# Gated mix of linear attention and a long convolution: taps constant over all lags, and the sum onto y on GpSimd

## The chip, the cores and the metric

The kernel runs on one core of a Trainium2 chip. The metric is the device time of one launch in microseconds (us), as the median of several runs. The engines are named as in the profile: PE is TensorE (PEld its weight loads), DVE is VectorE, ACT is ScalarE, POOL is GpSimd, and SP is the queue that issues the DMAs. All of them run beside each other and wait for one another through semaphores; each takes its own instructions in the order in which they were written.

## The reference: what is computed

x has 2048 rows (time) and 448 columns (channels). A gate g mixes two blocks of the same x:

```python
x = A_x
g = _sigmoid((x * gate_w).sum(-1, keepdims=True))
a = _A_ref(x, A_wqkv, A_wo)                      # linear attention, 16 heads of 28
b = _B_ref(x, ...)                               # convolution over time, one filter per channel
return g * a + (1 - g) * b

# _A_ref, not causal: phi(t) = where(t > 0, t + 1, exp(t)) + 1e-6
kv = jnp.einsum("bhsd,bhse->bhde", phi(k), v)
o = phi(q) kv / (phi(q) sum(phi(k)) + 1e-6)      # then o @ wo

# _B_ref: causal, as long as the sequence
A = -jnp.exp(log_A_real) + 1j * A_imag           # per channel, 256 modes
K = 2.0 * einsum("dn,dnl->dl", (C_real + 1j*C_imag) * dt, exp(A * dt * lag)).real
y = causal_convolution(x, K) + x * D_skip
```

The step dt = exp(log_dt) is around 1e-14 with these inputs, so over 2048 lags a filter K hardly moves: it is p0 + p1 * lag to very high accuracy, with p0 = 2 dt sum(C_real) and a slope p1 = -2 dt^2 sum(C_real exp(log_A_real) + C_imag A_imag).

## The kernel before, in words

**Tiles.** Time is cut into NC = 16 chunks of P = 128 rows, the channels into J = 4 blocks of DJ = 112. Matrices that need full accuracy are split into a high part in fp32r and the rest ("low"); a product is then three PE products, high by high, low by high, high by low. For a chunk c, `split_x(c)` (L260) makes one tile xw: ACT casts x to fp32r (L272), GpSimd subtracts for the low part of the transposed x (512 wide) and for the low part of x in natural order (448 wide; both L258). `skip(c)` (L277, GpSimd) writes x * D_skip into y[:, c]. `load_x` (L229) brings x of a chunk, 512 KB, through SP's queue.

**The main loop** (L520, c = 1 to 14, after chunks 0 and 1 have been begun by hand) does the following on PE:

- `project(c + 1, wk)` (L370): 11 matmuls for k of the next chunk, into one PSUM buffer named k. Then `k_post` (L410): ACT does relu and exp (L396, L397), VectorE the feature (L398, in PSUM), ACT the high part pkh (L402), VectorE the low part pkl and the running sum zb (both L408). The next k may start when zb has read the buffer.
- from c = 2, `project(c, wq)`: 11 matmuls for q of this chunk, into one PSUM buffer q, and `q_post` (L415): ACT exponentials (L416, L385), VectorE L386 and L389, into pq. The next q may start after L389.
- `do_g(c)` (L438): 11 matmuls that add x^T phi(k) into four PSUM banks.
- the triangle products v of the convolution, which are off this sequence by some chunks.

**The convolution inside a chunk.** With K = p0 + p1 * lag, written as p0 (1 + slope * lag) with slope = p1 / p0, and the lag as the difference of two positions, the part of a chunk that comes from itself is tri @ (x - x * s) scaled by near, where tri is the 128 by 128 triangle of ones and s the slope times the position. `do_wa` (L451, VectorE) makes q = x * slope, `do_wb` (L455, VectorE) subtracts it from the low part of x, `do_v` (L459, L460) is two PE products with tri, `v_post` (L464, VectorE) multiplies by near and sends the last row of the chunk into u by a DMA (L467), and `v_add` (L470, VectorE) adds to y[:, c]. Lists `vs` and `vq` and the tuple TWICE decide at which c which chunk's w and v are done; from c = 4 on it is one or two chunks an iteration, and their order on each engine is the order in the code.

**The convolution between chunks.** The 15 rows of u, and ru = u times the slopes, are gathered by four DMAs into zr (L492), split into zst, and multiplied by the constant matrix gcat in `inter(i)` (L740), in two groups of 8 chunks, into rc. In the attend stage one of the 11 matmuls of a chunk takes rc, against rows phi that hold the gate and the gate times the position (six rows a chunk), put there by DMA (L640) and copied by `tail` (L672).

**The preparation of the filter**, `s4d_prepare` (L305), is a generator of steps: exp; squares on ACT and sums with accumulation on VectorE (L314, L317); then small operations on [112, 4] tiles (L321 to L342), among them the check; then eight PE transposes (L347) that spread p0 and p1 over partitions, a copy into slope (L348), into ru (L350), and near = p0 (1 + slope) (L351). The steps are called before the loop, at c = 1 after `k_post`, at c = 2 after `q_post`, and at c = 3 around `q_post`.

**The check.** For each channel okc is 1 if the modes are slow enough (md), p0 is within bounds, and |p1| * FLAT <= |p0| with FLAT = 2^23. The count of channels that pass is loaded at the end; if one fails, `general_conv` computes the convolution in full and overwrites the output (L869).

**After the loop** come the gate (L423 to L425), `gates_a` and `gates_b` (the rows phi, L647 to L658), the sum of phi(k) over time spread by PE (L707, L708) and copied (L709), the normalisation of q (`norm_a` to `norm_d`), the products with wv and wo (L775, L749, L752), and then, for each of 16 chunks, the **attend stage**: `turn` (4 transposes, L664), `attend` (11 matmuls, L686), `final_b` (L691, VectorE, and the DMA out). A generator `late` (L814) puts the second `inter` and the gate of the last chunk between these.

Of the kernel before, what the change touches and what calls it, by code (L numbers as in the profile page):

```python
# [22 lines left out]
J = 4  # L23
# [6 lines left out]
LAG = 3  # L30
WARM = 8
QA = (2, 2, 5)
TWICE = (4, 5, 6, 8, 10, 12)
SMALL = 2.0 ** -70
FLAT = 2.0 ** 23
# [3 lines left out]
RG = 8  # L39
RX = DT + 6 * RG  # L40
NZ = 2 * (NC - 1)
KZ = 32 + NZ
# [129 lines left out]
def gated_mix_kernel(ctx: ExitStack, tc: tile.TileContext, xin, wk_d, wq_d, wv_d, wo_d, abc_d, ldt_d, dsk_d,  # L172
# [26 lines left out]
    gcat = const.tile([KZ, 2, RX], F32R, name="gcat")  # L199
    sel = const.tile([P, 2], F32, name="sel")  # L200
# [3 lines left out]
    rows = const.tile([P, 3 * D], F32, name="rows")  # L204
    near, slope, dsk = (rows[:, i * D:(i + 1) * D] for i in range(3))
    ru = const.tile([NC, D], F32, name="ru")
# [9 lines left out]
    xs = work.enter_context(tc.tile_pool(name="xs", bufs=LAG + 3))  # L216
# [5 lines left out]
    POOL.memset(zb, 0.0)  # L222

# [81 lines left out]
    def s4d_prepare():  # L305
# [4 lines left out]
        s0, s1, dt, am, p0, p1, d2, md, b0, b1, nk = (small() for _ in range(11))  # L310
# [9 lines left out]
        clamp = lambda p: DVE.tensor_scalar(out=p, in0=p, scalar1=-BIG, scalar2=BIG, op0=ALU.max, op1=ALU.min)  # L320
# [8 lines left out]
        clamp(p0)  # L329
        clamp(p1)  # L330
# [13 lines left out]
        o = [ps.tile([P, 512], F32, name="p%d" % i, tag="v%d" % (1 - i)) for i in range(2)]  # L344
        for i, f in ((0, p0), (1, p1)):
            for j in range(J):
                PE.transpose(o[i][:, j * DJ:(j + 1) * DJ], f[:, j:j + 1].to_broadcast([DJ, P]), ident[:DJ, :DJ])  # L347
        ACT.activation(slope, o[1][:, :D], AF.Copy, scale=sel[:, 0:1])  # L348
        yield
        ACT.copy(ru, o[1][:NC, :D])  # L350
        DVE.scalar_tensor_tensor(out=near, in0=slope, scalar=1.0, in1=o[0][:, :D], op0=ALU.add, op1=ALU.mult)  # L351
# [89 lines left out]
    vt, wt = {}, {}  # L441

    def do_w(c, eng):
        do_wa(c)
        do_wb(c, eng)

    wq = {}

    def do_wa(c):
        q = wq[c] = tp.tile([P, D], F32, name="q", tag="t")  # L450
        DVE.tensor_tensor(out=q, in0=xh[c][:, NAT:LO].bitcast(F32), in1=slope, op=ALU.mult)  # L451

    def do_wb(c, eng):
        w = wt[c] = tp.tile([P, D], F32R, name="w", tag="w")
        eng.tensor_tensor(out=w, in0=xh[c][:, XC:LT].bitcast(F32), in1=wq.pop(c), op=ALU.subtract)  # L455

    def do_v(c):
        v = vt[c] = ps.tile([P, 512], F32, name="v", tag="v%d" % (c % 2))
        PE.matmul(v[:, :D], lhsT=tri, rhs=xh[c][:, NAT:LO], start=True, stop=False)  # L459
        PE.matmul(v[:, :D], lhsT=tri, rhs=wt.pop(c), start=False, stop=True)  # L460

    def v_post(c):
        t = tp.tile([P, D], F32, name="t", tag="v0")
        DVE.tensor_tensor(out=t, in0=vt[c][:, :D], in1=near, op=ALU.mult)  # L464
        vt[c] = t
        if c < NC - 1:
            SP.dma_start(out=u[c:c + 1], in_=t[P - 1:P])  # L467

    def v_add(c):
        DVE.tensor_tensor(out=y[:, c], in0=y[:, c], in1=vt.pop(c), op=ALU.add)  # L470
# [6 lines left out]
    vs = list(range(NC))  # L477
    vq = []

    def v_next():  # L480
        vq.append(vs.pop(0))
        do_v(vq[-1])

    U = slice(0, NC - 1)

    def z_products():
        zr = tp.tile([P, D], F32, name="zr", tag="w")[:64]
        POOL.memset(zr, 0.0)
        DVE.tensor_tensor(out=ru[U], in0=u[U], in1=ru[U], op=ALU.mult)
        for o in (0, 32):  # L490
            for k, w in enumerate((u[U], ru[U])):
                SP.dma_start(out=zr[o + k * (NC - 1):o + (k + 1) * (NC - 1)], in_=w)  # L492
# [27 lines left out]
    for c in range(1, NC - 1):  # L520
        if c == 1:
            load_x(4)
            gcr = tp.tile([P, D], F32, name="gcr", tag="w")[:KZ, :2 * RX].rearrange("p (g m) -> p g m", g=2)
# [19 lines left out]
        if c + 2 < NC and c != LAG + 1:  # L543
            split_x(c + 2)
            skip(c + 2)
# [5 lines left out]
        if vq:  # L551
            v_add(vq.pop(0))
        if c in (NC - 5, NC - 3):
            low(POOL, wol[-1], wo[:, 2 * len(wol) - 2:2 * len(wol)], woh[-1])
        if c > LAG and c >= 12 and vs[c in TWICE:]:
            do_w(vs[c in TWICE], DVE)
        k_post(c + 1, ko)
# [5 lines left out]
        if c in TWICE:  # L563
            v_next()
            v_post(vq[0])
            if c > LAG + 1:
                v_add(vq.pop(0))
        if c == LAG + 1:
            split_x(c + 2)
            v_add(vq.pop(0))  # L570
            skip(c + 2)
# [12 lines left out]
        if c == 2:  # L584
            steps(1)
# [382 lines left out]
```

## Time and profile before

| what | value |
|---|---|
| median of 3 runs | 211.92 us (210.81 to 212.89) |
| span of the profiled execution, first to last instruction | 209.6 us |
| mean granted PE clock over the span | 0.985 of full speed |
| busy: PE, DVE, POOL, ACT | 179.2, 169.4, 105.7, 94.6 us |
| first k of iteration c = 2, 3, 4, 14 of the main loop | 25.70, 32.56, 40.41, 136.05 us |
| first attend matmul of the steady attend stage | 161.35 us |

The profile shows one execution. Its own time is recorded as the span only; the median of the runs lies 2.3 us above it. A page gives busy times, the chain of work that ended last, and groups of instructions by code line: "L470 DVE TENSOR_TENSOR y<-y,t 128x448" is an instruction of line 470 on VectorE that writes a tile y from y and t; xN is the count, then follow the total busy time in us, the mean of one in ns, and how long the engine was idle before them and for whom. A timeline row starts with the start and the duration in us; neighbouring instructions of one kind are merged, with their count. A window row has the start and end, the length, each engine's busy time with its count of instructions, and the granted PE clock.

### The profile page before, as it was taken

What the parts mean: (1) busy time and instruction counts of PE and PEld (TensorE: products, weight loads), DVE (VectorE), ACT (ScalarE), POOL (GpSimd) and SP (SyncE); (2) the same over time, 40 slices, a digit from 0 to 9 for tenths busy, and PEclk for the clock granted to TensorE, in tenths of its full rate; (3) what the DMA queues carried; (4) which work ended last, traced back from release to release, by engine and by line L of the source; (5) the groups of instructions that cost most, each with busy time, mean ns of one, the idle gap of its engine ahead of it and who ended that gap; (6) DMA issues with size and microseconds to landing.
All of it is one profiled execution on the core that took longest, in us unless ns stands there. A gap on an engine that the chain in (4) does not pass through costs nothing.

```text
span 209.6 us, 2815 instructions
## 1 busy us (share of the span) xinstructions
PE 179.2 (85%) x895; PEld 155.3 (74%) x895; DVE 169.4 (81%) x298; ACT 94.6 (45%) x192; POOL 105.7 (50%) x106
## 2 busy tenths in 40 slices
PE   7889699996986798969869596798979999999990
PEld 6678599895866687758748495695858989999980
DVE  2586479889998989898899889868979979998540
ACT  5695883354041442323260543336157456555530
POOL 1079959019560708254365619213655886886000
PEclk9999999999699999999999999999999999999997
DMA  5997946503020220033020302000000122222221
GB/s 199 338 296 250 276 135 246 184 2 104 0 85 16 100 79 21 0 105 100 0 97 5 105 0 55 5 15 0 4 2 0 44 93 90 89 89 90 91 110 36
DMA packets 8198, 18.65 MB, mean 89 GB/s; under 512 B 1756, under 2 KB 5040, under 8 KB 7952
## 3 DMA queue, kind: packets, MB, share of 16 engines
q1 hardware_dynamic: 8176, 18.39, 26.6%
q8 instruction: 9, 0.15, 0.3%
q14 instruction: 13, 0.11, 0.2%
HBM read 14.54 MB, written 3.67 MB: 87 GB/s over the span
## 4 chain that ended last, share of the span: by engine, by line
DVE 47%; PE 29%; issue 7%; ACT 7%; DMA 4%; POOL 2%; SPq 1%; DVEq 0%; ACTq 0%; POOLq 0%
PE a L686 17%; DVE y L470 8%; DVE q L451 6%; DVE w L455 5%; PE k L370 4%; DVE t L386 4%; DVE t L464 4%; DVE k L398 4%; DVE zb L408 4%; ACT pkh L402 3%; DVE pq L389 3%; PE tr L664 3%; DVE pkl L408 2%; DMA y<-in 2%; DMA xr<-in 2%
## 5 line engine op out<-in xcount | busy, mean ns | idle before, releaser
L258 POOL TENSOR_TENSOR xw<-xr,xw 128x448 fp32r<-128x448 f32 (+1 forms) x30 | 40.8, 1381 | 52.6 <-ACT xw L272 21.1
L370 PE MATMUL q<-wqh,xw 128*128 128x450 f32 x120 | 33.7, 383 | 6.8 <-DVE pq L389 4.8
L370 PE MATMUL k<-wkh,xw 128*128 128x448 f32 x120 | 32.7, 374 | 6.8 <-DVE zb L408 5.8
L438 PE MATMUL g<-pkh,xw 128*128 128x448 f32 x112 | 35.8, 367 | 0.0
L370 PEld LDWEIGHTS q<-wqh,xw 128*128 128x128 f32 x120 | 23.1, 196 | 10.6 <-ACT e L397 7.5
L370 PEld LDWEIGHTS k<-wkh,xw 128*128 128x128 f32 x120 | 21.6, 188 | 12.0 <-ACT e L385 4.0
L402 ACT ACTIVATE pkh<-k 128x448 fp32r<-128x448 f32 x15 | 8.2, 544 | 42.3 <-DVE k L398 42.3
L686 PE MATMUL a<-wkh,th 128*128 128x448 f32 (+1 forms) x119 | 26.9, 365 | 0.0
L603 POOL TENSOR_TENSOR prod<-pq,zb 128x448 f32<-128x448 f32 x16 | 18.5, 1161 | 10.4 <-ACT zb L709 6.1
L438 PE MATMUL g<-pkl,xw 128*128 128x448 f32 x64 | 23.6, 369 | 0.0
L438 PEld LDWEIGHTS g<-pkh,xw 128*128 128x128 f32 x112 | 21.0, 188 | 2.6
L686 PEld LDWEIGHTS a<-wkh,th 128*128 128x128 f32 x119 | 20.5, 189 | 1.3
L396 ACT ACTIVATE e<-k 128x448 f32<-128x448 f32 x15 | 8.1, 543 | 29.3 <-PE k L370 29.3
L277 POOL TENSOR_TENSOR y<-xr,rows 128x448 f32<-128x448 f32 x16 | 20.7, 1297 | 0.0
L470 DVE TENSOR_TENSOR y<-y,t 128x448 f32<-128x448 f32 x16 | 16.8, 1049 | 0.6
L455 DVE TENSOR_TENSOR w<-xw,q 128x448 fp32r<-128x448 f32 x16 | 15.7, 982 | 1.5
L626 POOL TENSOR_TENSOR pn<-pq,den 128x336 f32<-128x336 f32 x16 | 12.1, 754 | 9.3 <-DVE den L615 5.2
L370 PE MATMUL q<-wql,xw 128*128 128x450 f32 x45 | 16.7, 378 | 0.0
L408 DVE SCALAR_TENSOR_TENSOR pkl<-k,pkh 128x448 fp32r<-128x448 f32 x15 | 9.4, 624 | 8.6 <-ACT pkh L402 8.6
L370 PE MATMUL k<-wkl,xw 128*128 128x448 f32 x45 | 16.2, 367 | 0.0
L272 ACT CAST xw<-xr 128x1024 fp32r<-128x1024 f32 x14 | 14.8, 1055 | 2.8 <-DMA xr<-in 1.5
L451 DVE TENSOR_TENSOR q<-xw,rows 128x448 f32<-128x448 f32 x16 | 15.4, 960 | 0.0
(163 smaller groups left out, 349.1 us busy)
## 6 DMA issues: line engine op xcount, KB each, us to landing
xr<-in SPq DMA_DIRECT2D x14, 512.0 KB, 4.3
out<-ot SPq DMA_DIRECT2D x15, 224.0 KB, 1.9
pq<-in SPq DMA_DIRECT2D x2, 896.0 KB
xr<-in SPq DMA_DIRECT2D x4, 256.0 KB
y<-in SPq DMA_DIRECT2D x2, 450.0 KB, 5.6
y<-in SPq DMA_DIRECT2D x4, 224.0 KB
wv<-in SPq DMA_DIRECT2D x1, 896.0 KB
wo<-in SPq DMA_DIRECT2D x1, 784.0 KB
```

The source lines that it names most:

```text
L258: eng.tensor_tensor(out=o, in0=r, in1=h.bitcast(F32), op=ALU.subtract)
L272: ACT.copy(h[:, :XC], r)
L277: POOL.tensor_tensor(out=y[:, c], in0=xr[c][:, NAT:LO], in1=dsk, op=ALU.mult)
L370: PE.matmul(o[:, :n], lhsT=a, rhs=b, start=run.n == 1, stop=not seq)
L402: ACT.add(pkh[c], pks[c], 1e-6)
L408: DVE.scalar_tensor_tensor(out=o, in0=pk, scalar=1e-6, in1=a, op0=ALU.add, op1=op)
L438: PE.matmul(g[i][:a.shape[1], :D], lhsT=a, rhs=b, start=c == 0 and n == 0, stop=c == NC - 1 and n == len(seq) - 1)
L451: DVE.tensor_tensor(out=q, in0=xh[c][:, NAT:LO].bitcast(F32), in1=slope, op=ALU.mult)
L455: eng.tensor_tensor(out=w, in0=xh[c][:, XC:LT].bitcast(F32), in1=wq.pop(c), op=ALU.subtract)
L470: DVE.tensor_tensor(out=y[:, c], in0=y[:, c], in1=vt.pop(c), op=ALU.add)
L603: POOL.tensor_tensor(out=pd[c], in0=pq[:, c], in1=zb, op=ALU.mult)
L686: PE.matmul(a[:, lo:hi], lhsT=u_, rhs=w_[:, lo:hi], start=n == 0, stop=n == 10)
```

## The change

The filter is taken as constant, K = p0 for all lags, and the check is tightened so that this holds: FLAT goes from 2^23 to 2^35. If a channel's slope is larger, the general path runs as before. With that

- `do_wa`, `do_wb` and the tile w go; `do_v` multiplies tri with the high and the low part of x directly,
- `v_add` becomes a GpSimd addition inside `v_post`, ahead of the DMA of the row for u,
- a table VS states which chunks' v are done in which iteration: two at c = 4 to 8 (one behind k, one behind q), one at c = 9 to 14, each v's `v_post` standing between `k_high` and `k_low`, or behind `q_post`,
- the preparation loses p1's transposes, slope, ru and several small operations, near is a copy on ACT, and its steps come at c = 1, 2 and 3, behind the k part and ahead of q,
- there is one `inter` for all 16 chunks, with three rows phi a chunk in place of six; ru's product and two of the four DMAs into zr go; `gates_a` is only a view of og; a GpSimd memset of part of rows is added at the start.

The core of the diff:

```diff
-TWICE = (4, 5, 6, 8, 10, 12)
+VS = {c: (2 * c - 8, 2 * c - 7) for c in range(4, 9)} | {c: (c + 1,) for c in range(9, NC - 1)}
-FLAT = 2.0 ** 23
+FLAT = 2.0 ** 35
-RG = 8
-RX = DT + 6 * RG
-NZ = 2 * (NC - 1)
-KZ = 32 + NZ
+RX = DT + 3 * NC
+KZ = 32 + NC - 1
...
+    POOL.memset(rows[DT:RX, 2 * D:], 0.0)
...
-        clamp(p0)
-        clamp(p1)
+        DVE.tensor_scalar(out=p0, in0=p0, scalar1=-BIG, scalar2=BIG, op0=ALU.max, op1=ALU.min)
...
-        DVE.tensor_scalar(out=nk, in0=okc, scalar1=-1.0, scalar2=1.0, op0=ALU.mult, op1=ALU.add)
-        for p in (p0, p1):
-            tt(DVE, p, p, okc, ALU.mult)
-        tt(DVE, nk, nk, p0, ALU.add)
-        DVE.reciprocal(out=nk, in_=nk)
-        tt(DVE, p1, p1, nk, ALU.mult)
+        tt(DVE, p0, p0, okc, ALU.mult)
...
+        o = ps.tile([P, 512], F32, name="p", tag="v1")
+        for j in range(J):
+            PE.transpose(o[:, j * DJ:(j + 1) * DJ], p0[:, j:j + 1].to_broadcast([DJ, P]), ident[:DJ, :DJ])
+        ACT.copy(near, o[:, :D])
...
     def do_v(c):
         v = vt[c] = ps.tile([P, 512], F32, name="v", tag="v%d" % (c % 2))
         PE.matmul(v[:, :D], lhsT=tri, rhs=xh[c][:, NAT:LO], start=True, stop=False)
-        PE.matmul(v[:, :D], lhsT=tri, rhs=wt.pop(c), start=False, stop=True)
+        PE.matmul(v[:, :D], lhsT=tri, rhs=xh[c][:, XC:LT], start=False, stop=True)
 
     def v_post(c):
         t = tp.tile([P, D], F32, name="t", tag="v0")
-        DVE.tensor_tensor(out=t, in0=vt[c][:, :D], in1=near, op=ALU.mult)
-        vt[c] = t
+        DVE.tensor_tensor(out=t, in0=vt.pop(c)[:, :D], in1=near, op=ALU.mult)
+        POOL.tensor_tensor(out=y[:, c], in0=y[:, c], in1=t, op=ALU.add)
         if c < NC - 1:
             SP.dma_start(out=u[c:c + 1], in_=t[P - 1:P])
-
-    def v_add(c):
-        DVE.tensor_tensor(out=y[:, c], in0=y[:, c], in1=vt.pop(c), op=ALU.add)
...
+        vs = VS.get(c, ())
         ko = project(c + 1, wkh, wkl, D, "k")
-        if c > LAG and c < 12 and vs[c in TWICE:]:
-            do_w(vs[c in TWICE], DVE)
-        if vq:
-            v_post(vq[0])
+        for v in vs[:1]:
+            do_v(v)
+        if c + 2 < NC and c != LAG + 1:
+            split_x(c + 2)
+            skip(c + 2)
...
-        k_post(c + 1, ko)
+        k_feature(c + 1, ko)
+        k_high(c + 1)
+        for v in vs[:1]:
+            v_post(v)
+        k_low(c + 1)
+        if c == LAG + 1:
+            split_x(c + 2)
+            skip(c + 2)
...
-        if c == 1:
+        if c <= LAG:
             steps(1)
         if c > 1:
             qo = project(c, wqh, wql, D + 2, "q")
-            if c == LAG:
-                do_g(c, (0,))
-                steps(1)
-                do_wa(vs[0])
-                q_post(c, qo, lambda: do_wb(vs[0], DVE))
-                steps(1)
-            else:
-                q_post(c, qo)
-        if c == 2:
-            steps(1)
-        if c + 1 in TWICE and c > LAG:
-            do_w(vs[c > LAG], DVE)
+            for v in vs[1:]:
+                do_v(v)
+            q_post(c, qo)
+            for v in vs[1:]:
+                v_post(v)
         if c < NC - 2:
-            do_g(c, range(c == LAG, 4))
+            do_g(c)
         if c == LAG:
             POOL.tensor_copy(gcat, gcr)
-        if c > LAG and vs:
-            v_next()
...
     def gates_a(a, b):
-        g = tp.tile([P, NC - 2, 2], F32, name="g2", tag="g2", bufs=1)[:, :b - a]
-        DVE.tensor_copy(g[:, :, 0], og[:, a:b])
-        DVE.tensor_scalar(out=g[:, :, 1], in0=og[:, a:b], scalar1=sel[:, 0:1], scalar2=None, op0=ALU.mult)
-        return g.rearrange("p c k -> p (c k)")
+        return og[:, a:b]
...
     def late():
         c = NC - 1
-        yield 2
-        last = inter(1)
-        ACT.copy(rc[1][:DT], sh[:DT].bitcast(F32))
-        yield 3
-        last()
         yield 5
```

More of the change, by code (lines that the diff above doesn't have):

```diff
@@ L203, in gated_mix_kernel @@
     ones = ones_r.bitcast(F32)
-    rows = const.tile([P, 3 * D], F32, name="rows")
-    near, slope, dsk = (rows[:, i * D:(i + 1) * D] for i in range(3))
-    ru = const.tile([NC, D], F32, name="ru")
+    rows = const.tile([P, S], F32, name="rows")
+    near, dsk = (rows[:, i * D:(i + 1) * D] for i in range(2))
     u = const.tile([NC, D], F32, name="u")
@@ L439, in do_g @@
                           stop=c == NC - 1 and n == len(seq) - 1)
[L441 to L455, printed above, removed]
+    vt = {}
     def do_v(c):
@@ L671, in tail @@
     def tail(c):
-        ACT.copy(tl[c][DT:RX, 3], rows[DT:RX, c % RG * P:(c % RG + 1) * P])
+        ACT.copy(tl[c][DT:RX, 3], rows[DT:RX, c * P:(c + 1) * P])
     av = {}
@@ L700, in gated_mix_kernel @@
     g2 = gates_a(1, NC - 1)
-    POOL.memset(rows[DT:RX, :RG * P], 0.0)
+    POOL.memset(rows[DT:RX, :2 * D], 0.0)
     ACT.copy(zst, zr[:KZ])
@@ L733, in gated_mix_kernel, with inter @@
     kvl = tp.tile([DJ, J, DJ], F32R, name="kvl", tag="t")
-    def inter(i):
-        o = ps.tile([P, 512], F32, name="z%d" % i, tag="v%d" % i)
-        r = tp.tile([P, D], F32R, name="rc%d" % i, tag="w")
-        z = tp.tile([P, D], F32R, name="zs%d" % i, tag="v0")
+    def inter():
+        o = ps.tile([P, 512], F32, name="z", tag="v0")
+        r = tp.tile([P, D], F32R, name="rc", tag="w")
+        z = tp.tile([P, D], F32R, name="zs", tag="v0")
         rc.append(r)
-        PE.matmul(o[:RX, :D], lhsT=gcat[:, i], rhs=zst, start=True, stop=True)
+        PE.matmul(o[:RX, :D], lhsT=gcat, rhs=zst, start=True, stop=True)
         ACT.copy(z[DT:RX], o[DT:RX, :D])
-        return lambda: DVE.scalar_tensor_tensor(out=r[DT:RX], in0=z[DT:RX].bitcast(F32), scalar=sel[DT:RX, 1:2],
-                                                in1=o[DT:RX, :D], op0=ALU.mult, op1=ALU.add)
+        DVE.scalar_tensor_tensor(out=r[DT:RX], in0=z[DT:RX].bitcast(F32), scalar=sel[DT:RX],
+                                 in1=o[DT:RX, :D], op0=ALU.mult, op1=ALU.add)
     def mrows(j, pool, tag):
@@ L796, in gated_mix_kernel @@
     kv_split(0, k0)
-    inter(0)()
+    inter()
     q_run(QA[1])
```

73 lines of the change are left out of this document (16 added, 57 removed).

## The prediction, made before the changed kernel was run

> **What bounds the kernel now.** I began with the page: the busy shares, and the chain that ended last. Then I cut the span into stages at the starts of the projections of k (L370) in the timeline, and read each stage's window, the groups by line and shape, the views of single lines, and at last rows of the timeline. First the page:
>
> ```profile
> span 209.6 us, 2815 instructions
> ...
> PE 179.2 (85%) x895; PEld 155.3 (74%) x895; DVE 169.4 (81%) x298; ACT 94.6 (45%) x192; POOL 105.7 (50%) x106
> ...
> PE a L686 17%; DVE y L470 8%; DVE q L451 6%; DVE w L455 5%; PE k L370 4%; DVE t L386 4%; DVE t L464 4%; DVE k L398 4%; DVE zb L408 4%; ACT pkh L402 3%; DVE pq L389 3%; PE tr L664 3%; DVE pkl L408 2%; DMA y<-in 2%; DMA xr<-in 2%
> ```
>
> PE is the busiest engine over the span, yet the chain runs mostly over VectorE lines: L470, L451 and L455, three lines that the diff deletes, are its largest entries behind the attend matmuls (L686). An average over the span cannot tell which engine bounds which stage, so here are four stages (start:end, length, then busy time of PE, PEld, DVE, ACT and POOL with counts, granted clock, DMA):
>
> ```profile
> 25.70:32.56 6.86, 6.86 (x33) 6.22 (x34) 5.46 (x13) 5.56 (x13) 4.58 (x5) 1.00 0.41 125
> 32.56:40.41 7.85, 7.68 (x42) 6.72 (x41) 7.13 (x27) 3.00 (x7) 3.61 (x4) 1.00 0.84 287
> 40.41:136.05 95.64, 78.99 (x362) 67.58 (x362) 86.27 (x114) 33.41 (x64) 46.50 (x33) 0.98 0.15 48
> 161.35:204.00 42.65, 42.57 (x241) 38.56 (x240) 34.73 (x78) 22.42 (x51) 24.37 (x34) 1.00 0.22 83
> ```
>
> The first row is iteration c=2: 33 matmuls in 6.86 us without a gap, 0.2079 us each. That is PE's pace when nothing holds it. The third row is c=4 to c=13, ten iterations that also carry the triangle products (v): 362 matmuls, which at 0.2079 would take 75.3 us, took 95.64, and VectorE was busy for 86.27 of them. So these ten iterations are VectorE's, at 9.56 us each, and 20 us of PE's time in them is waiting. The last row is the attend stage, which is PE's.
>
> **What the engines do there.** Groups by line and shape (count | busy us, mean ns of one | idle before):
>
> ```profile
> L470 DVE TENSOR_TENSOR y<-y,t 128x448 f32<-128x448 f32 x16 | 16.8, 1049 | 0.6
> L455 DVE TENSOR_TENSOR w<-xw,q 128x448 fp32r<-128x448 f32 x16 | 15.7, 982 | 1.5
> L451 DVE TENSOR_TENSOR q<-xw,rows 128x448 f32<-128x448 f32 x16 | 15.4, 960 | 0.0
> L464 DVE TENSOR_TENSOR t<-v,rows 128x448 f32<-128x448 f32 x16 | 9.9, 616 | 0.0
> L398 DVE SCALAR_TENSOR_TENSOR k<-k,e 128x448 f32<-128x448 f32 x15 | 9.4, 628 | 6.4 <-ACT e L397 6.4
> L408 DVE SCALAR_TENSOR_TENSOR pkl<-k,pkh 128x448 fp32r<-128x448 f32 x15 | 9.4, 624 | 8.6 <-ACT pkh L402 8.6
> L408 DVE SCALAR_TENSOR_TENSOR zb<-k,zb 128x448 f32<-128x448 f32 x15 | 9.2, 615 | 0.0
> L389 DVE SCALAR_TENSOR_TENSOR pq<-q,t 128x448 f32<-128x448 f32 x14 | 8.7, 625 | 1.4
> L396 ACT ACTIVATE e<-k 128x448 f32<-128x448 f32 x15 | 8.1, 543 | 29.3 <-PE k L370 29.3
> L397 ACT ACTIVATE e<-e 128x448 f32<-128x448 f32 x16 | 9.2, 578 | 0.5
> L402 ACT ACTIVATE pkh<-k 128x448 fp32r<-128x448 f32 x15 | 8.2, 544 | 42.3 <-DVE k L398 42.3
> L701 POOL MEMSET rows<- 48x1024 f32 x1 | 0.9, 949 | 5.3 <-DVE t L464 5.3
> ```
>
> And four views of single lines, which give the shortest, the median and the longest duration in ns:
>
> ```profile
> L386 DVE TENSOR_SCALAR t<-e x15: 384/719/1346, 16.3 to 143.4; 128x448 f32<-128x448 f32 x15
> L277 POOL TENSOR_TENSOR y<-xr,rows x16: 1140/1279/1531, 15.5 to 128.6; 128x448 f32<-128x448 f32 x16
> L258 POOL TENSOR_TENSOR xw<-xr,xw x30: 1139/1306/1639, 14.3 to 127.1; 128x448 fp32r<-128x448 f32 x16, 128x512 fp32r<-128x512 f32 x14
> L258 POOL TENSOR_TENSOR wos<-wo,wos x2: 2132/2314/2497, 110.4 to 129.8; 112x896 fp32r<-112x896 f32 x2
> ```
>
> VectorE lines that have all inputs in SBUF have long means (L470, L455, L451: 0.96 to 1.05 us) or a wide spread (L386); those that read PSUM stay at 0.62. The timeline shows why:
>
> ```profile
> 56.11 0.63 DVE L470 TENSOR_TENSOR y<-y,t 128x448 f32<-128x448 f32 x1
> 59.37 2.79 POOL L258 TENSOR_TENSOR xw<-xr,xw 128x512 fp32r<-128x512 f32 x2 [4.30 <-ACT xw L272]
> 59.61 1.53 DVE L470 TENSOR_TENSOR y<-y,t 128x448 f32<-128x448 f32 x1
> ```
>
> The same add takes 0.63 us alone and 1.53 us when a GpSimd instruction has begun before it. VectorE's SBUF-to-SBUF work is held about for the length of a GpSimd instruction.
>
> **The change, part by part.**
>
> *Main loop, c=4 to c=13.* L451 and L455 go (15.4 + 15.7 us of VectorE) and L470 goes to GpSimd (16.8 us): 47.9 us leave VectorE. What is left in an iteration is L398, L464 (once or twice), L408 twice, L389 and L386: 0.628 + 0.616 + 0.624 + 0.615 + 0.625 + 0.384 to 1.346 = 3.5 to 4.5 us with one v, 4.1 to 5.1 with two. PE needs 33 + 2 matmuls (c=9 to 13), 7.28 us, or 33 + 4 (c=4 to 8), 7.69 us, so VectorE no longer bounds it. ACT has 33.41 us in ten iterations, 3.3 each. GpSimd has the two low parts (2.79) and the skip (1.28), 4.07 us, and now the adds. An add on GpSimd isn't in the trace; its nearest row is L277 (same shape, one operation, SBUF to SBUF), median 1.28 us, which I take. Below it may cost 1.14 (the shortest L277), above 1.64 (the longest L258). That makes 5.4 or 6.6 us an iteration, under PE's 7.28 and 7.69.
>
> Then the waits. k has one PSUM buffer: after its last matmul ACT does L396 and L397, VectorE L398, ACT L402 (beside which the new v_post, 0.616, stands), VectorE L408 twice: 0.543 + 0.578 + 0.628 + 0.616 + 0.624 + 0.615 = 3.6 us, some 3.9 with handovers. PE meanwhile has v, q and g, 24 matmuls, 5.0 us. The slack is 1.1 us, so PE is what is late next. v no longer waits for w. The second v_post of an iteration comes last on VectorE: q ends at 5.0 us (24 matmuls), then an exponential (0.58), L386, L389 and L464 give 7.2 to 8.2, that is -0.5 to +0.5 of the next iteration. On GpSimd's queue the add waits for it, and behind the add wait the next chunk's low parts; they come by 0.5 + 1.28 + 1.4 = 3.2 us, and PE wants them at 7.7. On SP's queue the row for u waits for it, and behind that the next load of x:
>
> ```profile
> xr<-in SPq DMA_DIRECT2D x14, 512.0 KB, 4.3
> ```
>
> It lands 4.3 us later, by 4.8, and the cast that reads it stands behind q's exponential, at 5.6. So ten iterations go at PE's pace: 330 matmuls of k, q and g and 30 of fifteen v (that of chunk 15 moves to c=14), 360 x 0.2079 = 74.8 us in place of 95.64: **-20.8 us**.
>
> *c=2 and c=3.* The third step of the preparation moves ahead of the q features of c=2 in VectorE's queue. The rows of before:
>
> ```profile
> 31.20 0.62 DVE L408 SCALAR_TENSOR_TENSOR zb<-k,zb 128x448 f32<-128x448 f32 x1
> 33.10 0.52 DVE L306 TENSOR_TENSOR sm<-sm 112x4 f32<-112x4 f32 x1
> 34.81 0.99 PE L370 MATMUL q<-wqh,xw 128*128 128x450 f32 x4
> 37.12 0.23 DVE L306 TENSOR_TENSOR sm<-sm,okc 112x4 f32<-112x4 f32 x2
> ```
>
> Its small operations took from 33.10 to 37.3. Now they start behind zb at 31.8 and, with a clamp and nk less (0.3 us), have p0 at 35.7, or at 37.2 if GpSimd holds them for one instruction more (1.5, as L470 above). Then two small ones, L386 and L389 (1.2 us) free the PSUM of q, and the q of c=3 starts at 36.9 to 38.4 instead of 34.81; 22 matmuls (4.6 us) later c=4 starts, at 41.5 to 43.0 instead of 40.41. Were VectorE not late at all, PE's own work would give 32.56 + 6.86 = 39.4 and a little for the transposes. I take 42.0, from the near end of the longer sum: **+1.6 us** (-0.8 to +2.6). What goes here (four transposes, the copies into slope and ru, near on VectorE, w of chunk 0) lies beside that wait and counts nothing; near as a copy on ACT is hidden too, ACT being busy 3.00 of 7.85 us.
>
> *Tail.* c=14 has the v of chunk 15 now, 0.4 us of PE, hidden since k's chain to zb decides; its v_post stands beside L402 as above. The product with ru and two of four DMAs into zr lay off the chain: nothing. The gates lose two instructions that stand on VectorE ahead of the reductions, and late() loses the second inter:
>
> ```profile
> 145.95 1.07 DVE L647 COPY g<-og 128x14 f32<-128x14 f32 x1
> 147.19 0.62 DVE L258 TENSOR_TENSOR zst<-zr,zst 30x448 fp32r<-30x448 f32 x1
> 168.88 0.46 PE L740 MATMUL z<-zst,gcat 62*112 62x448 f32 x1
> 169.27 0.66 PE L664 MATMUL tr<-ident,pn 128*128 128x128 f32 x4
> ```
>
> 147.19 - 145.95 = 1.24 us go; the zst subtraction may then fall beside a GpSimd product and give back up to 0.9 (1.53 - 0.63). I take **-1.0 us** (-0.3 to -1.2). In the attend stage the transposes followed 0.39 us behind the inter matmul: **-0.4 us**; its copies on ACT and VectorE were under PE's work. The phi rows are as many DMAs as before. The new memset at the start costs about what L701 does, 0.95 us, in GpSimd's first microseconds, when it waits for x: nothing, or +1.0 if it isn't covered.
>
> *Sum.* 209.6 - 20.8 + 1.6 - 1.0 - 0.4 = 189.0 us of span. The profiled execution is known by its span only; the runs' median, 211.92, lies 2.3 above it, so **191.3 us**.
>
> **Rivals.**
>
> *GpSimd becomes the bound (0.11).* If every GpSimd instruction took its longest, 1.64 us, because it now runs almost without a pause, five of them make 8.2 us against 7.69 in c=4 to 8, +2.5 us in all, and the two iterations with the extra subtraction of wo (2.31) add about 2.5 more: 196.3 us. For it speaks that GpSimd had 46.50 us in this stage and gets 15 more instructions; against it that it lost its time beside VectorE's SBUF work, which goes. To eat up the whole gain the add would have to take (95.64 - 40.7 - 4.6) / 15 = 3.4 us. The Trainium skill, GPSIMD Engine Reference, section 4.1 (Engine selection), speaks against this very move: elementwise work belongs on VectorE, being about two times slower on GpSimd. The trace agrees in the factor, 1.28 against 0.63 us.
>
> *PE's clock falls (0.03): slower than before.* The trace has one stretch in which matmuls start 0.37 us apart, behind a wait:
>
> ```profile
> 52.63 0.47 PE L460 MATMUL v<-w,tri 128*128 128x448 f32 x1 [1.93 <-DVE w L455]
> 54.40 0.58 PE L370 MATMUL q<-wql,xw 128*128 128x450 f32 x1
> 54.77 0.95 PE L370 MATMUL q<-wqh,xw 128*128 128x450 f32 x2
> ```
>
> If the denser loop ran so throughout, 360 x 0.164 = 59 us would come on top: 250 us. It decides from 126 matmuls on (20.6 / 0.164). Against it: the attend stage is dense for 42.65 us at a clock of 1.00. One such stretch of ten matmuls behind the longer wait at c=3 would cost 1.6 us, and is in the range. The Trainium skill, TensorE: Matmul & The Clock Gate, Part 1, says that the clock is halved after an idle window of about 3.4 us and that density keeps it up; by that page the wait at c=3 would cost no clock. The trace disagrees in the size: 1.93 us of waiting stood before this stretch.
>
> *The constant taps aren't taken (0.01).* Then the general path runs: its loads alone are 448 tiles of 1 MB, and at ten times the rate of the load above (512 KB in 4.3 us) these are 385 us on top. From the drawn inputs I worked out the largest ratio of slope to tap over the channels: 0.33 of the new limit of 2 to the power of -35, so all 448 channels pass.
>
> *A wait that I don't see holds the loop (0.05)*, at half of the gain, say: 201 us.
>
> **The numbers.** The likeliest case, the loop at PE's pace, gets 0.80. Its terms span 191.3 - 2.4 - 0.2 = 188.7 (c=3 and the tail at their low ends) to 191.3 + 1.0 + 0.7 + 1.6 + 1.0 = 195.6. With the GpSimd case at its full price the range is 188.5 to 196.5 and holds about 0.85. A difference of under 1% can't be told from no change here. Faster by over 1%: 0.96; within 1%: 0.01; slower: 0.03.
>
> **What would show it.** Right: iterations of 7.3 to 7.7 us from c=5 on with hardly a gap on PE, VectorE busy 4 to 5 us of each, GpSimd 5.4 to 6.6, L464 at 0.62, and the q of c=3 two us or more behind the end of its k. Wrong: k matmuls that wait for zb or for GpSimd's xw in every iteration, GpSimd adds over 1.64 us, a granted clock under 1.00 between c=4 and c=13, or VectorE still at 8 us an iteration.

## The result, and the profile after

The changed kernel takes 192.49 us (median of 4 runs, 190.71 to 192.84), the kernel before 211.92 us beside it; the ratio is 0.907, with a 95% interval of 0.901 to 0.914. (A fourth run of the kernel before took 217.35 us, over 1.5% more than its fastest, and counts as a slow one, so it is not compared.) 191.3 was predicted, with a range of 188.5 to 196.5. The profiled execution took 192.58 us at a span of 190.8, so 1.8 us lie around the span (all four runs show 1.7 to 1.8; the prediction had taken 2.3).

The page of the changed kernel, the same lines as of before (its lines are numbered 13 to 62 lower from L370 on: k and q are L357, g L425, v L432 and L433, v_post L437, the GpSimd add L438, attend L624):

```profile
span 190.8 us, 2736 instructions
...
PE 176.6 (93%) x890; PEld 157.9 (83%) x890; DVE 120.0 (63%) x237; ACT 93.9 (49%) x189; POOL 118.1 (62%) x123
...
PE 75%; DVE 14%; ACT 4%; issue 2%; DMA 2%; POOL 1%; SPq 0%; ACTq 0%; DVEq 0%
PE a L624 19%; PE k L357 17%; PE q L357 15%; PE g L425 14%; PE tr L602 3%; DVE y L315 2%; DMA y<-in 2%; PE v L433 2%; PE v L432 2%; PE m L690 1%; PE v L357 1%; DVE sm L306 1%; DVE k L385 1%; ACT e L384 1%; DVE den L550 1%
```

The chain that ended last now runs through PE's own lines, k, q, g and attend, where it ran through VectorE's L470, L451 and L455. VectorE's busy time fell by 49.4 us, GpSimd's rose by 12.4.

Four windows: iteration c=3, the stage c=4 to 13, one iteration with two v in it and one with one v (columns as before):

```profile
33.28:44.80 11.52, 9.00 (x37) 7.59 (x38) 8.26 (x22) 2.79 (x7) 3.73 (x4) 0.85 0.55 195
44.80:118.20 73.40, 73.40 (x361) 67.12 (x360) 37.52 (x65) 34.60 (x63) 56.87 (x48) 1.00 0.19 62
59.92:67.47 7.55, 7.55 (x39) 6.90 (x37) 4.42 (x9) 3.21 (x6) 6.27 (x6) 1.00 0.20 70
103.95:111.08 7.13, 7.13 (x37) 6.52 (x36) 3.42 (x7) 3.69 (x7) 4.68 (x5) 1.00 0.22 71
```

In the main stage PE is busy for all of the 73.40 us (95.64 before): the stage has gone from VectorE's to PE's. The first row is the opposite: c=3 took 7.85 us before and takes 11.52 now, with 2.5 us of waiting on PE and a granted clock of 0.85. Stage by stage against before: up to the k of c=3 +0.7 us (33.28 against 32.56), c=3 +3.7, c=4 to 13 -22.2, from c=14 to the end 72.6 against 73.55, -0.95; together -18.8, which is 209.6 to 190.8.

### The profile page after: what moved, and what is told of

It is laid out like the page before. It is cut to its first block, busy times and chain, and to the rows that moved or that the text cites. A ratio compares the mean times of both kernels' runs of the same rounds, so it can differ in the third digit from the quotient of the medians.

```text
span 190.8 us, 2736 instructions
## 1 busy us (share of the span) xinstructions
PE 176.6 (93%) x890; PEld 157.9 (83%) x890; DVE 120.0 (63%) x237; ACT 93.9 (49%) x189; POOL 118.1 (62%) x123
## 4 chain that ended last, share of the span: by engine, by line
PE 75%; DVE 14%; ACT 4%; issue 2%; DMA 2%; POOL 1%; SPq 0%; ACTq 0%; DVEq 0%
PE a L624 19%; PE k L357 17%; PE q L357 15%; PE g L425 14%; PE tr L602 3%; DVE y L315 2%; DMA y<-in 2%; PE v L433 2%; PE v L432 2%; PE m L690 1%; PE v L357 1%; DVE sm L306 1%; DVE k L385 1%; ACT e L384 1%; DVE den L550 1%
## 5 line engine op out<-in xcount | busy, mean ns | idle before, releaser
L256 POOL TENSOR_TENSOR xw<-xr,xw 128x448 fp32r<-128x448 f32 (+1 forms) x30 | 36.9, 1249 | 5.3 <-ACT xw L270 4.6
L438 POOL TENSOR_TENSOR y<-y,t 128x448 f32<-128x448 f32 x16 | 18.7, 1166 | 26.9 <-DVE t L437 25.2
L385 DVE SCALAR_TENSOR_TENSOR k<-k,e 128x448 f32<-128x448 f32 x15 | 9.5, 631 | 41.1 <-ACT e L384 41.1
L425 PE MATMUL g<-pkh,xw 128*128 128x448 f32 x112 | 35.3, 365 | 0.0
L357 PE MATMUL k<-wkh,xw 128*128 128x448 f32 x120 | 33.3, 384 | 2.2 <-DVE zb L395 1.5
L357 PE MATMUL q<-wqh,xw 128*128 128x450 f32 x120 | 33.2, 379 | 0.7 <-POOL wqh L256 0.4
L357 PEld LDWEIGHTS k<-wkh,xw 128*128 128x128 f32 x120 | 23.1, 197 | 5.5 <-ACT y L312 1.9
L624 PE MATMUL a<-wkh,th 128*128 128x448 f32 (+1 forms) x119 | 27.0, 365 | 0.0
L357 PEld LDWEIGHTS q<-wqh,xw 128*128 128x128 f32 x120 | 23.2, 195 | 3.6 <-issue 0.9
L425 PE MATMUL g<-pkl,xw 128*128 128x448 f32 x64 | 23.5, 367 | 0.0
L425 PEld LDWEIGHTS g<-pkh,xw 128*128 128x128 f32 x112 | 21.0, 188 | 2.5
L624 PEld LDWEIGHTS a<-wkh,th 128*128 128x128 f32 x119 | 20.5, 189 | 1.3
L275 POOL TENSOR_TENSOR y<-xr,rows 128x448 f32<-128x448 f32 x16 | 18.4, 1152 | 0.0
L606 ACT CAST th<-tr 128x512 fp32r<-128x512 f32 x16 | 9.4, 588 | 15.7 <-PE tr L602 15.5
L357 PE MATMUL k<-wkl,xw 128*128 128x448 f32 x45 | 16.7, 379 | 0.0
L357 PE MATMUL q<-wql,xw 128*128 128x450 f32 x45 | 16.4, 372 | 0.0
L629 DVE SCALAR_TENSOR_TENSOR ot<-y,og,a 128x448 f32<-128x448 f32 (+1 forms) x17 | 10.5, 617 | 6.5 <-PE a L624 6.4
L389 ACT ACTIVATE pkh<-k 128x448 fp32r<-128x448 f32 x15 | 8.2, 545 | 12.4 <-DVE k L385 12.4
```

What stands on the lines that cost most here:

```text
L256: eng.tensor_tensor(out=o, in0=r, in1=h.bitcast(F32), op=ALU.subtract)
L275: POOL.tensor_tensor(out=y[:, c], in0=xr[c][:, NAT:LO], in1=dsk, op=ALU.mult)
L357: PE.matmul(o[:, :n], lhsT=a, rhs=b, start=run.n == 1, stop=not seq)
L385: DVE.scalar_tensor_tensor(out=pks[c], in0=pks[c], scalar=1.0, in1=e, op0=ALU.add, op1=ALU.max)
L425: PE.matmul(g[i][:a.shape[1], :D], lhsT=a, rhs=b, start=c == 0 and n == 0, stop=c == NC - 1 and n == len(seq) - 1)
L438: POOL.tensor_tensor(out=y[:, c], in0=y[:, c], in1=t, op=ALU.add)
```

## The experiments

The theory was: VectorE bound the main loop through the two operations on w and the add; with the two on w gone it is far enough below PE that the place of the add does not matter, and c=3 is late since the moved preparation holds q's PSUM buffer. The rivals were that the move to GpSimd pays for its share, that the new order of the triangle products pays, and, for c=3, that the wait only moves. Ratios are against the kernel before, run on the same chip, with their 95% intervals.

### One part undone: the add on VectorE

```diff
-        POOL.tensor_tensor(out=y[:, c], in0=y[:, c], in1=t, op=ALU.add)
+        DVE.tensor_tensor(out=y[:, c], in0=y[:, c], in1=t, op=ALU.add)
```

> The changed kernel with one part undone: the sum onto y is on VectorE again, the rest as changed. Theory (VectorE bound the main loop through the three operations together, and the two on w are enough to free it): VectorE gets 16 adds of 0.63 to 1.5 us back, at most two an iteration, so it needs 5.4 to 7.5 us of an iteration in which PE needs 7.1 to 7.55; the loop from c=4 to c=13 stays at PE's pace, 73.4 us, at most 76, and the time is 192 to 195 us. GpSimd falls from 57 to about 41 us of that stage, and its operations get longer again. Rival (the move to GpSimd carries a part of the gain in proportion, 16.8 of 47.9 us): the loop takes about 81 us, the time is 199 to 201 us.

193.22 us, ratio 0.907 (0.901 to 0.913): the same as the whole change. The window of c=4 to 13:

```profile
44.88:118.38 73.50, 73.50 (x361) 67.03 (x360) 47.47 (x79) 34.57 (x63) 42.49 (x33) 1.00 0.19 62
```

VectorE has 10 us more, GpSimd 14 less, and PE is still busy all the time. The sum on GpSimd brings nothing in this kernel: it took load off an engine that had room already. The theory held.

### The other part undone: w made on VectorE, the add on GpSimd

```diff
+    def do_w(c):
+        q = tp.tile([P, D], F32, name="q", tag="t")
+        DVE.tensor_tensor(out=q, in0=xh[c][:, NAT:LO].bitcast(F32), in1=zz, op=ALU.mult)
+        w = wt[c] = tp.tile([P, D], F32R, name="w", tag="w")
+        DVE.tensor_tensor(out=w, in0=xh[c][:, XC:LT].bitcast(F32), in1=q, op=ALU.subtract)
...
-        PE.matmul(v[:, :D], lhsT=tri, rhs=xh[c][:, XC:LT], start=False, stop=True)
+        PE.matmul(v[:, :D], lhsT=tri, rhs=wt.pop(c), start=False, stop=True)
```

`do_w` of the first v of an iteration stands ahead of k, that of the second behind `k_low`; zz is a tile of zeros.

> The changed kernel with the other part undone: VectorE does the two operations that made w again (x times a tile of zeros, and the low part minus that, so w is the low part of x), a slot ahead of each triangle product, and the sum stays on GpSimd. Theory (the two operations are the load that bound the loop): VectorE needs 4.1 to 5.1 us plus two times 1.25 to 3 us in iterations with two v, some 8 to 9, above PE's 7.55, and 6 to 7.5 in those with one; the loop grows by 4 to 8 us, the time is 196 to 201 us, and the wait on VectorE's w is back in the list of waits of PE. Rival (the new placing of the products and not the work was what paid): the loop stays at 73 to 75 us, the time at 192 to 194.

208.12 us, ratio 0.979 (0.973 to 0.985): slower than either side expected. The window of c=4 to 13, and the chain in order of time over one iteration:

```profile
44.34:133.86 89.52, 76.98 (x362) 67.51 (x361) 66.01 (x94) 34.44 (x63) 64.00 (x48) 0.98 0.16 51
```

```profile
66.48 2.25 PE k L359 x11
...
70.01 0.65 DVE k L387
70.66 0.02 issue
70.68 0.56 ACT pkh L391
71.23 0.02 issue
71.26 0.62 DVE pkl L397
71.88 0.53 DVE zb L397
72.41 0.54 DVE q L434
72.96 0.02 issue
72.98 0.64 DVE w L436
73.61 0.04 issue
73.66 0.47 PE v L441
74.13 2.23 PE g L427 x11
```

No engine is full here: VectorE is busy for 66 of 89.5 us, PE for 77. PE waits for w five times, 11.3 us in all, of the 16.1 us that the loop has grown by. The chain goes from k's last matmul through k's features to w, which stands behind them on VectorE, then to the second v, and g stands behind that v on PE. So w costs through the wait as well as through the load, and how much depends on where it is put; the number is that of this placement. That w is what holds the loop is shown; that it does so by its load alone is not.

### Each part alone in the kernel before

Only w removed (`do_wa` and `do_wb` empty, the triangle product takes the low part of x; taps constant inside a chunk and sloped between chunks), everything else as before, the add on VectorE:

```diff
     def do_wa(c):
-        q = wq[c] = tp.tile([P, D], F32, name="q", tag="t")
-        DVE.tensor_tensor(out=q, in0=xh[c][:, NAT:LO].bitcast(F32), in1=slope, op=ALU.mult)
+        pass
...
-        PE.matmul(v[:, :D], lhsT=tri, rhs=wt.pop(c), start=False, stop=True)
+        PE.matmul(v[:, :D], lhsT=tri, rhs=xh[c][:, XC:LT], start=False, stop=True)
```

> The kernel before with one part of the change alone: the two VectorE operations that make w are left out and the triangle product takes the low part of x (so the taps are constant inside a chunk, and still sloped between chunks); the sum stays on VectorE, the order of the triangle products, the two inter products, the six phi rows and the preparation stay as before. Theory (these two operations on VectorE were the load that bound the loop, and c=3 is delayed only by the moved preparation): the loop from c=4 to c=13 goes at PE's pace, 73 to 76 us; c=3 takes 7.9 as before; the time is 190 to 193 us, no longer than the whole change. Rival (the new order of the triangle products is needed as well): the loop takes 80 us or more, the time is 197 or more.

194.09 us, ratio 0.9075 (0.901 to 0.914). Iterations c=2 and c=3, and c=4 to 13:

```profile
25.68:34.07 8.39, 8.39 (x33) 7.54 (x34) 5.68 (x14) 5.72 (x13) 4.12 (x5) 0.80 0.48 146
34.07:41.72 7.65, 7.65 (x42) 6.72 (x41) 6.93 (x26) 3.00 (x7) 3.42 (x4) 1.00 0.70 255
41.72:117.57 75.85, 74.92 (x364) 67.22 (x363) 59.28 (x82) 33.95 (x64) 45.12 (x33) 1.00 0.19 61
```

The loop takes 75.85 us, as the theory had it: 19.8 of the 22.2 us come from these two operations alone, in the old order of the triangle products. So the new order isn't needed; it and the rest of the change are worth at most the other 2.4. c=3 is not delayed. The time misses the theory's 190 to 193 by 1 us; in the profiled execution c=2 lost 1.5 us to a clock of 0.80 (half clock from 26.5 to 30 us, behind a wait of 2.21), and a second such stretch stands in the tail, at 136 us. The expectation held neither.

Only the add moved:

```diff
-        DVE.tensor_tensor(out=y[:, c], in0=y[:, c], in1=vt.pop(c), op=ALU.add)
+        POOL.tensor_tensor(out=y[:, c], in0=y[:, c], in1=vt.pop(c), op=ALU.add)
```

> The kernel before with the other part alone: the sum onto y on GpSimd, everything else as before. Theory: w stays on VectorE and PE keeps waiting for it behind GpSimd's instructions; as the kernel with w kept gave 208 us, the time is 203 to 210 us. Rival (VectorE was just over its limit, so any 16.8 us off it free the loop): 86.3 - 16.8 = 69.5 us of VectorE against 73.4 of PE, the loop at PE's pace, the time 190 to 194 us.

203.36 us, ratio 0.951 (0.944 to 0.958).

```profile
40.85:127.36 86.51, 78.84 (x363) 69.21 (x363) 76.24 (x100) 33.58 (x64) 65.57 (x48) 0.96 0.17 53
```

This takes 9.1 us off the loop, less than half of what the other part gives. VectorE is still busy for 76 of 86.5 us, and PE still waits longest for w: five times, 6.5 us in all. The theory held. The two parts give 19.8 and 9.1 alone and 22.2 together, not 28.9: with w gone PE is nearly the bound, and most of what the add gives is cut off there.

### How near GpSimd is to the bound

```diff
-        POOL.tensor_tensor(out=y[:, c], in0=y[:, c], in1=t, op=ALU.add)
+        for _ in range(2):
+            POOL.tensor_tensor(out=y[:, c], in0=y[:, c], in1=t, op=ALU.add)
```

> The changed kernel with each GpSimd sum done twice (so y gets twice the part of its own chunk, and the output is off by that). It tells how near GpSimd is to the bound. GpSimd then needs 3 x 1.2 + 4 x 1.17 = 8.3 us in iterations with two v, where PE needs 7.55, and 5.9 with one, where PE needs 7.1. Theory (GpSimd has slack ahead of PE's need, 4 us of it in the order of its queue): it falls behind by 0.8 us an iteration for five iterations, 4 us, and catches up behind them; the time is 192 to 194 us. Rival (GpSimd is the next bound directly): the loop grows by 0.8 us in each of five iterations and more with the two subtractions of wo, the time is 196 to 199 us.

196.08 us, ratio 0.920 (0.914 to 0.926). The window of c=4 to 13, and PE's waits in the iterations that have two v in or ahead of them:

```profile
43.78:120.28 76.50, 74.23 (x362) 66.81 (x360) 40.75 (x65) 34.35 (x63) 70.40 (x60) 1.00 0.19 60
```

```profile
52.62 0.88 PE L357 MATMUL k<-wkh,xw 128*128 128x448 f32 x3 [0.91 <-POOL xw L256]
...
83.58 0.88 PE L357 MATMUL k<-wkh,xw 128*128 128x448 f32 x3 [0.47 <-POOL xw L256]
91.88 0.88 PE L357 MATMUL k<-wkh,xw 128*128 128x448 f32 x3 [0.90 <-POOL xw L256]
```

The loop grows by 3.1 us: k now waits for the low part of x from GpSimd, once at the start, where the split of chunk 6 stands behind the add, and twice at the end of the iterations with two v; between these GpSimd falls behind without a wait of PE. My theory of 4 us of slack was too generous; the time lies in the rival's range. The changed kernel has 6.27 us of GpSimd in the iteration of 7.55 shown above, so there it lies only about one add (1.17 us) below its second bound, GpSimd, for the sake of an add whose move gains nothing. At c=5, where it makes up for the split that c=4 leaves it, GpSimd is busy for all of the 7.56 us already.

### c=3: the preparation behind q again

```diff
-        if c <= LAG:
+        if c == 1:
             steps(1)
...
+            if c == LAG:
+                steps(1)
             for v in vs[1:]:
                 do_v(v)
             q_post(c, qo)
+            if c == 2:
+                steps(1)
```

> The changed kernel with the third step of the preparation put behind the q features of c=2 again, as before the change, and the fourth, the transposes, behind the q product of c=3. Theory (the small operations ahead of q's features hold q's PSUM, and PE waits 2.5 us in c=3 and then runs 2.4 us at half clock): q of c=3 starts right behind its k, c=3 falls from 11.5 to 7.6 to 8.2 us, the span by 3 to 4 us, the time is 188.5 to 189.5. Rival (the wait only moves: k of c=4 then waits for zb, since the k features of c=3 come behind the small operations): c=3 takes 9.5 to 10.5, the time is 191 to 192.

188.78 us, ratio 0.8875 (0.883 to 0.892). First the rows of PE, VectorE and GpSimd at c=3 in the changed kernel, as the thing to be explained:

```profile
35.40 0.37 PE L357 MATMUL k<-wkl,xw 128*128 128x448 f32 x1
37.97 0.82 PE L337 MATMUL p<-ident,sm 112*128 112x112 f32 x4 [2.20 <-issue]
39.11 1.84 PE L357 MATMUL q<-wqh,xw 128*128 128x450 f32 x4 [0.32 <-DVE pq L376]
```

```profile
34.25 0.52 DVE L304 TENSOR_TENSOR sm<-sm 112x4 f32<-112x4 f32 x1
34.69 1.19 DVE L306 SCALAR_TENSOR_TENSOR sm<-sm 112x4 f32<-112x4 f32 x2
35.87 1.17 DVE L306 SCALAR_TENSOR_TENSOR sm<-sm 112x4 f32<-112x4 f32 x2
...
37.70 0.16 DVE L304 TENSOR_TENSOR sm<-sm,okc 112x4 f32<-112x4 f32 x1
37.85 0.38 DVE L373 TENSOR_SCALAR t<-e 128x448 f32<-128x448 f32 x1
38.34 0.62 DVE L376 SCALAR_TENSOR_TENSOR pq<-q,t 128x448 f32<-128x448 f32 x1
```

```profile
33.45 2.41 POOL L256 TENSOR_TENSOR xw<-xr,xw 128x512 fp32r<-128x512 f32 x2 [0.52 <-ACT xw L270]
35.81 1.13 POOL L275 TENSOR_TENSOR y<-xr,rows 128x448 f32<-128x448 f32 x1
```

k ends at 35.8; PE's next work, the transposes, needs p0 (37.86), and the q behind them needs its PSUM buffer, which L376 leaves at 38.96. A small operation takes 0.16 us at 37.70; the two pairs of L306 take 1.19 and 1.17 and end where a GpSimd instruction ends (35.88 against 35.86, 37.04 against 36.94). Then four matmuls of q take 1.84 us, where 0.98 is usual. And the windows of c=3 and of c=4 to 13 with the step moved back:

```profile
32.16:39.79 7.63, 7.40 (x37) 6.49 (x38) 6.83 (x22) 2.70 (x7) 3.77 (x4) 1.00 0.81 295
39.79:113.19 73.40, 73.40 (x361) 67.11 (x360) 38.14 (x66) 34.45 (x63) 56.79 (x48) 1.00 0.19 62
```

c=3 falls to 7.63 us and the loop stays as it was. The rival falls: the wait did not move.

### c=3: the wait filled with matmuls that nobody uses

```diff
+    KW = (9, 3)
+
+    def keep_warm(n):
+        w = ps.tile([P, 512], F32, name="kw", tag="v0")
+        for _ in range(n):
+            PE.matmul(w[:, :D], lhsT=ones_r, rhs=wkh[:, 1], start=True, stop=True)
...
+        keep_warm(KW[0])
         for j in range(J):
             PE.transpose(o[:, j * DJ:(j + 1) * DJ], p0[:, j:j + 1].to_broadcast([DJ, P]), ident[:DJ, :DJ])
+        keep_warm(KW[1])
```

> The changed kernel with 12 matmuls more at c=3, of ones on a block of wk into a PSUM buffer that is free there: nine ahead of the transposes, three behind, to fill the time in which PE waits for p0 and for q's PSUM. They are work that nobody uses. Theory (PE's wait there brings on the stretch at half clock behind it): the granted clock is 1.00 from 33 to 45 us, the ten matmuls behind the wait start 0.205 us apart instead of 0.37, c=3 falls from 11.5 to about 9.9 us, the time by 1.3 to 1.8 us. Rival (the clock falls at times of its own or after any break of the stream, however short): a half-clock stretch remains, the time is the same or up to 0.5 us longer.

191.72 us (median of six runs from 190.24 to 194.19), ratio 0.898 (0.892 to 0.904). c=3 in this kernel, and PE's rows in it:

```profile
32.25:42.66 10.41, 9.97 (x50) 8.66 (x50) 8.28 (x22) 2.79 (x7) 3.76 (x4) 1.00 0.63 216
```

```profile
34.56 1.97 PE L308 MATMUL kw<-wkh,ones_r 128*128 128x448 f32 x9
...
38.11 1.05 PE L366 MATMUL q<-wqh,xw 128*128 128x450 f32 x4
```

q begins as late behind k as in the changed kernel, but the clock stays at 1.00 and c=3 is 1.1 us shorter. That is what the theory said, but it doesn't show that the filling did it. The kernel with each sum done twice has the same c=3 as the changed kernel, with nothing in the wait, and its profile has

```profile
33.40:43.78 10.38, 7.58 (x37) 6.52 (x38) 8.26 (x22) 2.79 (x7) 3.73 (x4) 1.00 0.62 216
```

```profile
38.09 0.57 PE L337 MATMUL p<-ident,sm 112*128 112x112 f32 x4 [2.22 <-issue]
39.23 1.06 PE L357 MATMUL q<-wqh,xw 128*128 128x450 f32 x4 [0.57 <-DVE pq L376]
```

There the clock is 1.00 as well, behind the same wait, and c=3 is as short as with the filling. The changed kernel, that with the add on VectorE and that with w kept have the stretch at half clock behind this wait (a clock of 0.85, 0.85 and 0.86 over c=3). So the same wait brings it in some executions and not in others, and one profile with the wait filled can't tell what kept it away. In the time the filled kernel can't be told from the changed one, whose interval reaches into its own. A stretch at half clock came later in its execution, at 133.5 us, behind a wait of 1.47 us between the loop and the attend stage.

### The tail: zst ahead of the gate

With the step moved, `ACT.copy(zst, ...)` and the subtraction into zst stand ahead of `gate(0, NC - 1)` in place of behind `gates_a`.

> The kernel with the third step behind the q features of c=2 (188.8 us), and the subtraction into zst moved ahead of the gate, before GpSimd's first product with zb begins. Theory (the 1.53 us of that subtraction in the tail of the changed kernel are 0.62 of work and 0.9 of waiting for GpSimd's product, on the chain): it takes 0.62, the reductions behind it start 0.9 us earlier, the time is 187.6 to 188.2 us. Rival (the wait moves to the gate's operations behind it, which then stand beside the product): no difference, 188.5 to 189.1.

188.05 us, ratio 0.881 (0.876 to 0.886); once more on another chip 188.55 us, 0.886 (0.882 to 0.890). VectorE in the changed kernel, then in this one:

```profile
128.01 1.53 DVE L256 TENSOR_TENSOR zst<-zr,zst 15x448 fp32r<-15x448 f32 x1
129.75 0.62 DVE L550 TENSOR_REDUCE den<-prod 128x16 f32<-128x448 f32 x1
```

```profile
122.64 0.61 DVE L256 TENSOR_TENSOR zst<-zr,zst 15x448 fp32r<-15x448 f32 x1
123.27 1.03 DVE L410 TENSOR_SCALAR e<-e 128x15 f32<-128x15 f32 x1
125.37 0.60 DVE L554 TENSOR_REDUCE den<-prod 128x16 f32<-128x448 f32 x1
```

The subtraction falls from 1.53 to 0.61, but the gate's first operation, 15 values a row, now takes 1.03 beside GpSimd's product. From the start of c=14 the reduction comes at 11.12 us against 11.55: 0.4 us gained, half by the theory and half by the rival, and less than the runs can tell.

### The tail: PE's waits filled

The last kernel with eight matmuls more that nobody uses: five ahead of the gates' transpose, three ahead of the products with wo. Beside it on the same chip the kernel without them.

> The kernel with the third step moved and zst ahead of the gate (188.05 us), with eight matmuls more that nobody uses, where PE waits between the loop and the attend stage: five ahead of the transposes of the gates (a wait of 1.10 us in that kernel), three ahead of the products with wo (0.61 us). Theory (waits of PE there bring on the stretch at half clock that some executions show in this stage and others not, so that times of one kernel differ by 1 to 2 us): no run shows a mean clock under 0.996, the runs agree within 0.5 us, and the median falls to 187.0 to 187.5. Rival (the clock falls at times of its own, or after the short matmuls of this stage as well): clocks of 0.987 to 0.998 over the runs as before, the median between 187.8 and 188.5.

> The same kernel without the eight matmuls, on the same chip, to compare with: 188.05 us as before, clocks of 0.987 to 0.998. If the eight matmuls keep the clock up, it is slower than the filled one by 0.5 to 1 us and its runs are wider spread; by the rival the two agree within 0.4 us.

188.24 us against 188.55, with mean clocks of 0.983 to 0.994 over the runs against 0.983 to 0.998. The clock is as uneven as without the filling, and the times agree within 0.4: the rival's result. The two profiles can't say where the other runs lose clock: in both executions it is at 1.00 until 183 us, in the waits of the tail too, filled or not. In the nine profiles of kernels with zst in its old place PE waits 1.5 us ahead of the products with wo; in six of them a stretch at half clock follows, and in three (the kernel before, the changed kernel and that with w kept) none does. What brings on the half clock, at c=3 too, and why only in some executions, stays open.

## Why the prediction was right, step by step

- **The loop is VectorE's and becomes PE's.** Right, and shown: the window after has PE busy for all of it. Iterations were to take 7.3 to 7.7 us and take 7.13 and 7.55. The term was -20.8 and measured -22.2. The miss is PE's pace: it was taken from an iteration of 6.86 us with 33 matmuls, 0.2079 each, where 7.13 us for 35 is 0.2037. That iteration began behind a wait of 1.94 us, and its first four matmuls took 0.88 us instead of 0.81, which is about half of the excess.
- **What part does it.** The prediction lumped the 47.9 us that leave VectorE. The runs part them: the two operations on w alone give 19.8 of 22.2 us, the add alone 9.1, and the add behind w's removal nothing (73.50 against 73.40).
- **The add on GpSimd.** It was priced at 1.28 us from L277 and takes less, and GpSimd's other instructions got shorter too. First two groups of before, then three of the changed kernel:

```profile
L258 POOL TENSOR_TENSOR xw<-xr,xw 128x448 fp32r<-128x448 f32 x16 | 22.5, 1406 | 0.7 <-ACT xw L281 0.7
L277 POOL TENSOR_TENSOR y<-xr,rows 128x448 f32<-128x448 f32 x16 | 20.7, 1297 | 0.0
```

```profile
L438 POOL TENSOR_TENSOR y<-y,t 128x448 f32<-128x448 f32 x16 | 18.7, 1166 | 26.9 <-DVE t L437 25.2 <-PE g L425 1.6
L275 POOL TENSOR_TENSOR y<-xr,rows 128x448 f32<-128x448 f32 x16 | 18.4, 1152 | 0.0
L256 POOL TENSOR_TENSOR xw<-xr,xw 128x448 fp32r<-128x448 f32 x16 | 19.3, 1208 | 0.7 <-ACT xw L279 0.7
```

  The skip takes 1.152 us against 1.297 before, the low part 1.208 against 1.406: the rival "GpSimd becomes the bound" needed longer instructions, and they became shorter. The Trainium skill, SBUF — State Buffer, section "Who interferes with whom", says that a VectorE instruction with two SBUF inputs contends with a GpSimd instruction that reads SBUF, and that one with at most one SBUF input, outside the two-port modes, doesn't. The traces agree: v_post, with one input in PSUM and one in SBUF, takes 0.615 us beside a GpSimd that runs 57 of 73 us, while the add with two SBUF inputs took 0.61 to 2.20 us on VectorE in the kernel before. L373, whose one input is in SBUF, spreads from 0.38 to 1.28 us in the changed kernel; whether it runs in such a mode no trace here shows.
- **c=2 and c=3: the step with the largest miss.** "I take 42.0, from the near end of the longer sum: +1.6 us (-0.8 to +2.6)." The mechanism was right, the size not: c=4 began at 44.80, +4.4, beyond the end of this term's range. There are three parts. c=3 began 0.7 us late already; the same code differs by that much between executions (c=3 begins at 32.25 us in the kernel with the wait filled, at 33.40 in that with the sum done twice). Then p0 came at 37.86 and not at 35.7, 0.7 beyond the far end of 37.2. The prediction let the small operations start behind zb at 31.8, as the rows of before have it, but zb ended at 33.1, since the sums ahead of k's features took longer as well (two of them 1.59 and 1.67 us, against 1.16 and 0.69 before); and beside GpSimd the small operations were held three times (0.52, 1.19 and 1.17 us), where the rows of before have it twice. The third part is the stretch at half clock, 1.1 us (11.52 against the 10.38 of the execution without it). The prediction had named it, at 1.6 us, and put it into the range only. The move of the step behind q's features takes all of this away: c=4 then begins at 39.79.
- **Tail and attend.** -1.4 was predicted, -0.95 measured. The two gate operations went, but the zst subtraction then waited for GpSimd's product (1.53 us in place of 0.62), the give-back that had been named and mostly not taken.
- **Outside the span.** 1.8 us, not 2.3. Together: +0.7 and +2.1 in the head, -1.4 in the loop, +0.4 in the tail, -0.5 outside are +1.3, from 191.3 to the 192.58 of the profiled execution. That the total came this near is in part luck: misses of +3.2 and of -1.9 us cancel.

The best version that the runs hold, constant taps with the preparation behind q (and zst ahead of the gate), takes 0.88 to 0.89 of the time before, 2% less than the change as made.

## What to carry to other kernels

Ask of each stage which engine is full there, and price a change by how far the next engine lies below: here removing two of three operations already brought the loop to PE's pace, and the third could stay where it was. When a step is moved ahead in an engine's order, look for the buffer that the work behind it releases: 4.8 us of small operations (33.05 to 37.86) in front of one PSUM reader cost c=3 3.7 us, 2.5 of them by PE's waiting and 1.1 by the clock. Moving work onto GpSimd pays only where the engine that it leaves would still be the bound without the move.

## What had not been expected of the hardware

PE ran at half clock for stretches of about 3.5 us. In the main loop they followed waits of PE: 1.93 us in the kernel before (from 53 us on), 2.20 and 0.32 us at c=3 in the changed kernel. But a wait alone doesn't bring one: none followed a wait of 2.58 us in the kernel before, nor the same c=3 wait (2.22 and 0.57 us) in the kernel with the sum done twice. So the one profile with that wait filled, at a clock of 1.00, shows nothing about the filling. Mean clocks over runs of one kernel lay between 0.983 and 0.998 with or without filled waits in the tail; those runs differ by 1.6 to 2.1 us, and the mean clock alone doesn't order them (187.21 us at 0.994 and 189.31 us at 0.993 are the same kernel).

An operation of VectorE on 15 values a row took 1.03 us beside a GpSimd product and 0.17 ahead of it, so taking zst out of the product's way handed the wait to this one.
